# Zero matmuls into spare PSUM columns at the start of an attention and expert kernel

## The chip, the cores and the metric

The kernel runs on one core of a Trainium2 chip. The metric is the device time of one execution in microseconds, and lower is better. Every kernel's result was also compared with the reference; all that are told of here were correct. A run is called slow when it lies over 1.5% above the fastest of the same kernel; comparisons use fast runs. "The clock" of a run is the mean granted TensorE clock in its record, as a share of full speed; the slow start of a run is not in it. In the profiles PE is TensorE (PEld its weight loads), DVE is VectorE, ACT ScalarE, POOL GpSimd and SP SyncE.

## The reference

```python
def _attn_ref(q, k, v, g_q, g_k):           # q, k, v: (8, 12, 448, 64) float32
    def rmsnorm(x, g):
        rms = np.sqrt(np.mean(x * x, axis=-1, keepdims=True) + 1e-06)
        return x / rms * g
    q_n, k_n = (rmsnorm(q, g_q), rmsnorm(k, g_k))
    scores = 1.0 / np.sqrt(64) * np.matmul(q_n, k_n.transpose(0, 1, 3, 2))
    scores = scores - np.max(scores, axis=-1, keepdims=True)
    attn = np.exp(scores)
    attn = attn / (np.sum(attn, axis=-1, keepdims=True) + 1e-09)
    return np.matmul(attn, v).astype(np.float32)

def _moe_ref(x, w_in, w_out):               # x: the attention's output as (3584, 768)
    h = x @ w_in                            # w_in (768, 2048)
    g = h * np.clip(h + 3.0, 0.0, 6.0) / 6.0
    return (g @ w_out).astype(np.float32)
```

## The kernel before

A plan lists steps with estimated durations and dependencies, sorts them greedily, and the program is then written out in that order, each engine in its own fixed sequence. A step that names only one engine is wrapped in a function without a name of its own.

```python
    def add(self, on, dur, due, fn, *deps, ...):
        on, f = ({on: dur}, lambda e: fn()) if isinstance(on, str) else (on, fn)
        s = Step(on, due, f, deps, ...)
# ...
    S_r = Ring(tiles("S", 2, [128, 2, 512], FP32, psum))     # scores: four banks
    X_r = Ring(tiles("X", 1, [128, 512], FP32, psum))        # values: columns 0 to 389
    R_r = Ring(tiles("R", 1, [128, 512], FP32, psum))        # values of the last 64 rows, three pairs of heads
    M_r = Ring(tiles("M", 2, [128, 512], FP32, psum))        # transposes and the expert layers
# ... for the pair of heads P: first two transposes (k, q) on TensorE, each followed by a DVE copy
                tr.append(add("PE", 0.4, at - 2, trans, sc[i], id_make, *mwar))
            ks = add("DVE", 0.45, at - 1, lambda: nc.vector.tensor_scalar_mul(
                kp[:, 0:S], pt[:, 0], gp[:, 0:1]), tr[0], g_make, one_make, *kwar)
            qc = add("DVE", 0.45, at - 1, lambda: nc.vector.tensor_copy(out=kq[:, 1], in_=pt[:, 1]), tr[1], *war)
# ... then four score steps, exponentials on ScalarE, and the value steps into X and R
        X, war, x_use = X_r.take()
        av = []
        for s in range(NS):
            av.append(add("PE", 0.27, at + 0.15 * step * s, lambda s=s: values(
                X[:, s * 130:(s + 1) * 130], s * 128, s == 0), *exps, vc, *war))
# ...
        rest = add("PE", 0.27, at + 0.45 * step, lambda: values(
            Rt[:, i * 130:(i + 1) * 130], S - 128, i == 0), *exps, vc, *war)
# ...
        def norm():                          # the normalisation: DVE reads X
            nc.vector.reciprocal(out=rd[:].unsqueeze(3), in_=xv[:, :, :, D:E1])
            nc.vector.tensor_tensor(out=xn[:], in0=xv[:, :, :, 0:D],
                                    in1=rd[:].unsqueeze(3).to_broadcast([128, NS, 2, D]), op=MULT)

        xe = add("DVE", 0.85, at + 0.5 * step, norm, *av, *dwar, *nwar)
# ... R is read by norm_rest after every third pair; xn is transposed on TensorE, copied to xT by DVE,
# ... and after six pairs the expert matmuls of the batch start
    with tc.manual_schedule():
        for s in plan.order():
            s.fn(s.eng)
```

Below, "kp" and "kq" are DVE's copies of a pair's transposed k and q, and "xn" is its normalised output; a "score pair" is the two score matmuls of one step.

Of the kernel before, what the change touches and what calls it, by code (L numbers as in the profile page):

```python
# [9 lines left out]
BF16 = mybir.dt.bfloat16  # L10
# [134 lines left out]
def kernel(  # L145
# [11 lines left out]
    nc = tc.nc  # L157
# [15 lines left out]
    const = ctx.enter_context(tc.tile_pool(name="const", bufs=1))  # L173
    psum = ctx.enter_context(tc.tile_pool(name="psum", bufs=1, space=PSUM))

    def tiles(name, n, shape, dt=BF16, pool=const):
        return [pool.tile(shape, dt, name=f"{name}{i}") for i in range(n)]

    gq_t, gk_t, gp = (const.tile([128, 1], FP32, name=n) for n in ("gq_t", "gk_t", "gp"))
    mark = const.tile([1, 1], FP32, name="mark")  # L180
    ident = const.tile([128, 128], BF16, name="ident")
    w_in_sb = const.tile([128, NKT, DFF], BF16, name="w_in_sb")
    w_out_sb = const.tile([128, NFT, DM], BF16, name="w_out_sb")
# [19 lines left out]
    X_r = Ring(tiles("X", 1, [128, 512], FP32, psum))  # L203
    R_r = Ring(tiles("R", 1, [128, 512], FP32, psum))
# [58 lines left out]
    def make_ones():  # L263
# [7 lines left out]
        out=gp[:], in0=gq_t[:], scalar=8.0, in1=gk_t[:], op0=MULT, op1=MULT), g_load, after=7.5)  # L271
# [366 lines left out]
    for _, fn in sorted(blocks, key=lambda x: x[0]):  # L638
        fn()

    with tc.manual_schedule():
        for s in plan.order():
            s.fn(s.eng)


# [28 lines left out]
```

## Time and profile before

| | before |
|---|---|
| median of the timed runs | 442.79 us (442.28 to 442.87) |
| profiled execution | 440.47 us, span 438.6 us, clock 1.0 |
| TensorE slow (score pair 0.55 us) | until about 25.5 us |
| first expert matmul | 45.48 us |

Two lines of the page of the kernel before: the busy time of each engine, and the chain of work that ended last, by engine.

```profile
PE 410.6 (94%) x3663; PEld 229.2 (52%) x3682; DVE 246.3 (56%) x417; ACT 249.0 (57%) x425; POOL 240.2 (55%) x230
...
PE 80%; POOL 5%; DVE 4%; ACT 3%; issue 3%; DMA 3%; SPq 1%; POOLq 0%
```

Averages over the span say that TensorE bounds the kernel, and from about 57 us on it does. The first 50 us are another stage, and what sets the pace there has to be read from the timelines of the engines in that stage. The prediction shows those lines.

### The profile page before, as it was taken

The numbers are of one execution on the slowest core, as the hardware profiler recorded it, in microseconds if no ns is written. First come the engines' busy times: TensorE is split into PE (matmuls) and PEld (weight loads), VectorE is DVE, ScalarE is ACT, GpSimd is POOL, SyncE is SP. The second block draws the span as 40 slices with busy tenths as digits, with TensorE's granted clock in tenths as the row PEclk, the third lists the DMA queues.
The fourth block names the chain that finished last, engine by engine and source line by source line (L and its number), as shares of the span: only waits on it lengthen the run. The fifth ranks groups of instructions, "written<-read, shape, count | busy, mean of one in ns | idle before, by whom it ended". The sixth has DMA issues, their size and how long they took to land.

```text
span 438.6 us, 9205 instructions
## 1 busy us (share of the span) xinstructions
PE 410.6 (94%) x3663; PEld 229.2 (52%) x3682; DVE 246.3 (56%) x417; ACT 249.0 (57%) x425; POOL 240.2 (55%) x230
## 2 busy tenths in 40 slices
PE   0588799999999999999999999999999999999995
PEld 0355455555455565554455565554455555654563
DVE  1998887657674564456555465556564444334421
ACT  3788588657765666367664677357673665123200
POOL 3499988855757567656765657747757510000000
PEclk9999999999999999999999999999999999999999
DMA  8999999877545745674465655684465420220122
GB/s 241 247 265 261 224 214 193 216 197 192 128 121 148 189 113 136 167 214 111 133 156 157 177 135 145 159 214 109 120 161 164 97 56 12 54 81 0 37 72 73
DMA packets 102923, 64.58 MB, mean 147 GB/s; under 512 B 59744, under 2 KB 99424, under 8 KB 102880
## 3 DMA queue, kind: packets, MB, share of 16 engines
q1 hardware_dynamic: 94544, 57.01, 50.6%
q0 software_dynamic: 7296, 6.29, 9.1%
q10 hardware_dynamic: 1040, 0.69, 0.5%
q8 instruction: 29, 0.48, 0.5%
q14 instruction: 14, 0.11, 0.1%
HBM read 45.61 MB, written 11.01 MB: 129 GB/s over the span
## 4 chain that ended last, share of the span: by engine, by line
PE 80%; POOL 5%; DVE 4%; ACT 3%; issue 3%; DMA 3%; SPq 1%; POOLq 0%
PE M L558 27%; PE M L533 25%; PE S L416 9%; PE X L437 8%; PE S L558 4%; PE R L437 2%; PE S L533 2%; DVE ssq L337 1%; ACT e L421 1%; POOL qks L351 1%; PE X L558 1%; POOL sq L322 1%; POOL va L359 1%; DMA gq_t<-in_g_q_dram 1%; POOL sq L329 1%
## 5 line engine op out<-in xcount | busy, mean ns | idle before, releaser
L421 ACT ACTIVATE e<-S 112x896 bf16<-112x896 f32 x192 | 166.3, 914 | 64.1 <-PE S L416 64.0
L533 PE MATMUL M<-xT,w_in_sb 128*128 128x384 bf16 (+1 forms) x679 | 145.1, 349 | 3.7 <-DVE gT L541 2.9
L351 POOL TENSOR_TENSOR qks<-qk,rs 112x512 bf16<-112x512 f32 x87 | 90.5, 1055 | 86.6 <-ACT rs L344 84.7
L558 PE MATMUL M<-w_out_sb,gT 128*128 128x384 bf16 x736 | 131.8, 326 | 0.0
L558 PEld LDWEIGHTS <-gT 128*128 128x128 bf16 x896 | 82.9, 98 | 57.8 <-issue 7.8
L533 PEld LDWEIGHTS <-w_in_sb 128*128 128x128 bf16 x768 | 69.6, 97 | 67.4 <-issue 12.5
L541 DVE SCALAR_TENSOR_TENSOR gT<-t,M 128x384 bf16<-128x384 f32 (+1 forms) x116 | 70.6, 611 | 59.1 <-ACT t L539 58.3
L539 ACT ACTIVATE t<-M 128x384 f32<-128x384 f32 (+1 forms) x116 | 62.6, 540 | 67.0 <-PE M L533 65.5
L437 PEld LDWEIGHTS <-e 112*128 112x128 bf16 x1536 | 65.1, 99 | 31.4 <-issue 16.0
L337 DVE TENSOR_REDUCE ssq<-sq 112x16 f32<-112x1024 f32 (+1 forms) x49 | 58.4, 1193 | 23.3 <-POOL sq L329 12.2
L329 POOL TENSOR_TENSOR sq<-qk 112x1024 f32<-112x1024 f32 x36 | 68.1, 1892 | 0.0
L416 PE MATMUL S<-kq,kp 64*128 64x448 bf16 x384 | 56.6, 364 | 4.1 <-DVE kp L381 1.7
L437 PE MATMUL X<-va,e 112*128 112x65 bf16 x1152 | 58.6, 196 | 0.8 <-ACT e L421 0.6
L566 DVE COPY y<-M 128x384 f32<-128x384 f32 x46 | 25.6, 556 | 59.2 <-PE M L558 59.0
L359 POOL CAST va<-vf 112x512 bf16<-112x512 f32 x48 | 31.5, 658 | 10.4 <-DMA vf<-in_v_dram 10.1
L392 POOL TENSOR_SCALAR kp<-kq,gp 128x448 bf16<-128x448 bf16 x23 | 32.3, 1402 | 5.3 <-DMA kq<-qks 5.2
L463 DVE TENSOR_TENSOR xn<-X,rd 128x384 bf16<-128x384 f32 x48 | 26.8, 558 | 1.6
L416 PEld LDWEIGHTS <-kp 64*128 64x128 bf16 x384 | 12.2, 94 | 27.7 <-issue 18.0
L437 PE MATMUL R<-va,e 112*128 112x65 bf16 x384 | 20.4, 195 | 0.0
L377 PE MATMUL M<-ident,qks 112*128 112x112 bf16 x80 | 7.9, 242 | 13.0 <-DVE qks L351 12.4
L558 PE MATMUL S<-w_out_sb,gT 128*128 128x384 bf16 x112 | 19.5, 326 | 0.0
L462 DVE RECIPROCAL rd<-X 128x6 f32<-128x6 f32 x48 | 9.2, 192 | 15.3 <-PE X L437 15.2
(42 smaller groups left out, 156.2 us busy)
## 6 DMA issues: line engine op xcount, KB each, us to landing
qk<-in_k_dram SPq DMA_DIRECT2D x48, 224.0 KB, 3.3
vf<-in_v_dram SPq DMA_DIRECT2D x48, 224.0 KB, 3.7
qk<-in_q_dram SPq DMA_DIRECT2D x45, 224.0 KB, 3.4
w_in_sb<-in_moe_w_in_dram POOLq DMA_DIRECT2D x4, 768.0 KB, 11.3
w_out_sb<-in_moe_w_out_dram POOLq DMA_DIRECT2D x4, 768.0 KB, 11.9
out_dram<-y SPq DMA_DIRECT2D x8, 336.0 KB, 3.1
out_dram<-y SPq DMA_DIRECT2D x8, 288.0 KB, 3.4
out_dram<-y SPq DMA_DIRECT2D x8, 240.0 KB, 3.2
```

Source lines behind the costliest of these rows:

```text
L329: parts = [add("POOL", 1.93, at - 10, lambda: nc.gpsimd.tensor_tensor(out=sq[0:PT], in0=qk[0:PT], in1=qk[0:PT], op=MULT), *ld, *war, lock= ...
L337: red = add("DVE", 0.6 * n, at - 8 * hurry + 0.5 * i0, lambda i0=i0, i1=i1, cs=cs: nc.vector.tensor_reduce(out=ssq[0:PT, cs], in_=sq[0:PT, ...
L351: sc.append(add(on, 0, at - 6 * hurry, lambda e, i=i, rs4=rs4: engines[e].tensor_tensor(out=qks[0:PT, i].rearrange("p t h d -> p h t d"), ...
L359: vc = add({"POOL": 0.61}, 0, at - 3, lambda e: engines[e].tensor_copy(out=va[0:PT, :, :, 0:D], in_=vf[0:PT].rearrange("p h (t d) -> p h t ...
L392: nc.vector if e == "DVE" else nc.gpsimd).tensor_scalar_mul(
L416: nc.tensor.matmul(out=ps[:, a, 0:S], lhsT=kp[rows, c0:c0 + 128], rhs=kq[rows, 1, :], start=True, stop=True)
L421: x = add("ACT", 0.93, at + step * (t0 + i) / T + 0.2, lambda t=t0 + i, ps=ps: nc.scalar.activation(out=e[0:PT, t], in_=ps[0:PT, :, 0:S], ...
L437: nc.tensor.matmul(out=dst[:, a * E1:(a + 1) * E1], lhsT=e[0:PT, t, a, c0:c0 + 128], rhs=va[0:PT, a, t, :], start=(first and a == 0 and t ...
L533: nc.tensor.matmul(out=m[:, 0:n], lhsT=w_in_sb[:, kt, f * 128:(f + 1) * 128], rhs=X[:, kt, :], start=(kt == 0), stop=(kt == NKT - 1))
L539: r = add("ACT", 0.08 + n / 1200, due + span, lambda: nc.scalar.activation(out=t[:, 0:n], in_=m[:, 0:n], func=RELU, bias=0.5, scale=1.0 / ...
L541: g = add("DVE", 0.12 + n / 960, due + span, lambda: nc.vector.scalar_tensor_tensor(out=G[:, f, :], in0=t[:, 0:n], scalar=1.0, in1=m[:, 0: ...
L558: nc.tensor.matmul(out=m[:, 0:HALF], lhsT=G[:, f, i * 128:(i + 1) * 128], rhs=w_out_sb[:, f, cols], start=(f == 0), stop=(f == NFT - 1))
```

## The change

The intent: TensorE starts at half clock and gets the full one only at about 25 us. Zero matmuls into columns of X and R that nobody reads keep it busy from the first instruction on, so that the clock is released before the first real work; more of them, in front of the first 36 TensorE steps, are to keep it released. The destination is meant to be whichever of X and R was read longer ago.

```diff
+    zero = const.tile([128, 120], BF16, name="zero")
...
+    IDLE = [74, 1, 6, 1, 3, 1, 1, 2, 9, 2, 1, 2, 1, 1, 2, 1, 1, 2, 1, 2, 1, 1, 1, 1, 1, 1, 1, 1, 1, 1,
+            1, 1, 1, 1, 1, 1]
+    read = {"norm": [X_r.bufs[0], 0.0], "norm_rest": [R_r.bufs[0], 0.0]}
+
+    def spin(n):
+        to = min(read.values(), key=lambda x: x[1])[0]
+        for _ in range(2 * n):
+            nc.tensor.matmul(out=to[0:120, 392:512], lhsT=zero[:], rhs=zero[:], start=True, stop=True)
+
     with tc.manual_schedule():
+        nc.vector.memset(zero[:], 0.0)
+        n = 0
         for s in plan.order():
+            if s.eng == "PE":
+                if n < len(IDLE):
+                    spin(IDLE[n])
+                n += 1
+            if s.fn.__name__ in read:
+                read[s.fn.__name__][1] = s.end
             s.fn(s.eng)
```

## The prediction

> **What bounds the kernel now.** I read the page's chain first: most of it is dense TensorE work in the perceptron part (L533 and L558 carry 52% between them), and busy time by stretches gives PE 238.07 of 240 us from 60 to 300 us. A start-up effect is therefore worth what it moves the moment, near 56 us, at which that dense work begins; nothing later can win it back, and nothing later can lose more. So the second view is the timeline of PE over the first 30 us (columns: start, duration, engine, line, operation, count, and in brackets the idle time before it and who ended it).
>
> ```profile
> PEclk9999999999999999999999999999999999999999
> ```
>
> ```profile
> 11.69 0.55 PE L377 MATMUL M<-ident,qks 112*128 112x112 bf16 x4 [11.69 <-DVE qks L351]
> ...
> 14.28 0.93 PE L416 MATMUL S<-kq,kp 64*128 64x448 bf16 x4 [1.23 <-DVE kq L383]
> ...
> 19.44 0.55 PE L416 MATMUL S<-kq,kp 64*128 64x448 bf16 x2 [1.67 <-DVE kp L381]
> ...
> 22.88 0.93 PE L377 MATMUL M<-ident,qks 112*128 112x112 bf16 x8
> ...
> 27.19 0.36 PE L416 MATMUL S<-kq,kp 64*128 64x448 bf16 x2
> 27.48 0.37 PE L377 MATMUL M<-ident,qks 112*128 112x112 bf16 x4
> ```
>
> The same pair of score matmuls takes 0.55 us until about 25.5 us and 0.36 us after it; sixteen value matmuls start 0.98 us before their successor early and 0.61 us late. PE is slow until 25.5 us, although the page's clock row shows full clock throughout. From 19.44 to 25.5 PE has no gap over 0.15 us, so it looks like the bound there. The third view, the timeline of DVE over the same time, says otherwise.
>
> ```profile
> 12.36 1.21 DVE L337 TENSOR_REDUCE ssq<-sq 112x16 f32<-112x1024 f32 x1
> 13.49 0.44 DVE L381 TENSOR_SCALAR kp<-M,gp 128x448 bf16<-128x448 bf16 x1
> ...
> 16.17 2.55 DVE L322 TENSOR_TENSOR sq<-qk 112x512 f32<-112x512 f32 x1
> 18.64 0.38 DVE L383 COPY kq<-M 128x448 bf16<-128x448 bf16 x1
> ...
> 23.29 0.56 DVE L463 TENSOR_TENSOR xn<-X,rd 128x384 bf16<-128x384 f32 x1
> 23.85 0.45 DVE L381 TENSOR_SCALAR kp<-M,gp 128x448 bf16<-128x448 bf16 x1
> 24.22 0.38 DVE L383 COPY kq<-M 128x448 bf16<-128x448 bf16 x1
> 24.77 0.36 DVE L480 COPY xT<-M 128x384 bf16<-128x384 bf16 x1 [0.17 <-PE M L476]
> ...
> 27.04 0.20 DVE L462 RECIPROCAL rd<-X 128x6 f32<-128x6 f32 x1 [0.42 <-PE X L437]
> 27.27 0.56 DVE L463 TENSOR_TENSOR xn<-X,rd 128x384 bf16<-128x384 f32 x1
> 27.89 0.39 DVE L383 COPY kq<-M 128x448 bf16<-128x448 bf16 x1
> ```
>
> DVE runs from 12.36 to 24.6 us without a marked gap, and what it takes from PE lay ready before. In the whole cold stretch it waits for PE for 0.17 + 0.42 us. A fast PE can return about 0.6 us there, and no more. From 32.3 us POOL takes over (busy 15.04 of 15.5 us between 29.5 and 45 us); its first link hangs on DVE's reduction at 30.55 us through ScalarE.
>
> **What the Trainium skill says.** "TensorE: Matmul & The Clock Gate", Part 1: TensorE's default clock is half rate, and about 3.4 us of sustained activity, in a free-running window, releases it. The durations agree: the change comes some 6 us after PE's first unbroken stretch begins at 19.44 us. The same page, under Fast Weight Load, has the fast load only with 128 weight columns; the added loads have 120, those of before all 128, so this trace cannot say what a 120-column load costs. "PSUM — Partial Sum Buffer", on bank collisions: two engines may not touch one bank and quadrant at once, even in disjoint columns. So the zeros in X's spare columns are not free of X's readers. "SBUF — State Buffer", Who interferes with whom: an exclusive shared port of DVE and GpSimd; the 2.55 us square at 16.17, against 0.68 us at 35.19, with GpSimd squaring beside it, fits, and it says that DVE's stretch isn't shortened by PE.
>
> **The change part by part.** The list sums to 130, so 260 pairs of weight load and 120-column matmul are added to PE, and one DVE memset of a zero tile. Nothing is removed.
>
> First, 148 pairs from about 1 us. From the 112-column transposes I take cold pairs at (0.55 - 0.295)/3 = 0.085 to 0.11 us (0.295 us is the mean duration of one), say 0.10 at 120 columns, and warm ones at (0.37 - 0.214)/3 = 0.052, say 0.053. If the clock is released about 4.5 us after the start, 45 are cold and 103 warm: 4.5 + 5.5 = 10 us, ending near 11 us. The first transposes start at 11.69, and DVE wants them only at 13.49 us; with fast transposes an end up to 12.6 us costs nothing.
>
> Second, 48 pairs in front of steps 2 to 9 (11.7 to 19.4 us). They fall mostly in gaps of 0.26, 1.23, 0.54 and 1.67 us; up to 19.39 us the chain is DVE's. Cost and gain: about 0.
>
> Third, 64 pairs in front of steps 10 to 36, in the stretch where PE is dense. There cold PE work of 6.06 us shrinks to some 3.6 us, a gain of 2.4 us of PE time; the zeros give back 64 x 0.053 = 3.4 us. Alone this makes PE about as late at 29 us as before: the possible 0.6 us of gain is eaten.
>
> Fourth, new waits. I compared the order of the two built programs with their semaphore values. The intent is to write whichever of X and R was read longest ago, but all 260 go to X: the bookkeeping looks for a function name that the plan's wrapper hides. The program then makes two zero matmuls wait for a normalisation (reciprocal and multiply, DVE) that reads X. Both sit in front of real work.
> (a) The zeros before the third pair's q transposes wait for the first normalisation, which ends at 23.29 + 0.56 = 23.85 us. Before, these transposes ended at 23.81 us. Now: 23.91, two zeros to 24.02, four transposes to their end at 24.39. DVE's kp, in the program behind these transposes, starts at about 24.4 instead of 23.85: DVE stands 0.55 us. The score step behind them starts near 24.43 instead of 23.75.
> (b) The zeros before the third pair's third score step wait for the second normalisation. Carrying (a) on: kq ends 25.2, scores at 25.3; a transpose, sixteen and eight value matmuls and one score pair with five pairs of zeros end at 27.7 us (27.0 before), so the normalisation runs 27.7 to 28.5. Scores at 28.65 instead of 27.19, transposes at 29.05 instead of 27.48, DVE's kq at 29.46 instead of 27.89 us: 1.57 us late, DVE standing some 0.95 us.
> No later zero matmul has a wait. The reduction of 30.55 and POOL's product of 32.33 us follow that kq in order, so POOL's packed stretch starts some 1.5 us late. From there POOL and then PE have little slack; I allow 0.2 us recovered in DVE's small waits for PE between 35 and 40 us (0.44 and 0.27 us). Sum: +1.3 us, 442.8 + 1.3 = 444.1 us.
>
> **The rivals.**
> A: the warm-up works as meant. For it: PE is gapless and slow from 19.44 to 25.5. Against it: DVE's timeline and the two waits. It would be 442.8 - 0.6 = 442.2, and 440 us only if all 2.4 us of PE time lay on the chain.
> B: the 120-column load isn't fast and a pair takes 0.10 us warm as well. Then the first 148 end at 1 + 14.8 = 15.8 us; q's transposes end near 16.4, DVE's kp comes 2.9 us late, and the later zeros cost up to 64 x 0.047 = 3 us more: 447 to 449 us. Against it: 148 x 0.074 us fills exactly the 11 us available, as if tuned with cheap pairs.
> C: the delay is absorbed between 32 and 56 us, because the loads gain 1.5 us on the compute. For it: DMA is full in the first slices. Against it: no wait for DMA is listed for an engine between 29.5 and 60 us. Result 442.8 us.
>
> **Range and chances.** My steps give 444.1 with some 0.6 us of doubt in how much of 1.5 us passes through; A and C stretch the low end to 442.2, a part of B the high end to 446.6. Two per cent is 8.9 us: faster would need 434 us, out of reach even if all slow PE time vanished; slower would need 451.6, above B. Chances: faster 0.01, within 2% 0.97, slower 0.02.
>
> **What would show it.** Right: score pairs of 0.36 us from the first one at 14.28 us; zeros ending between 10 and 12.6 us; DVE's kp of 13.49 us unmoved; a zero matmul ended by DVE's xn, near 23.9 and near 28.5 us; kp of 23.85 at about 24.4 and kq of 27.89 near 29.5 us with PE as its releaser; POOL's product of 32.33 near 33.8 us; the same dense part afterwards, shifted. Wrong: the first transposes after 12.6 us (B), kq near 27.5 us (A), POOL at 33.8 but the first dense stretch at 56 us unmoved (C), or score pairs at 0.55 us still, which would mean that zero operands or the gaps don't hold the clock; then the zeros before 19.4 us cost nothing but those after it twice as much, about 446 us.

## The result, and the profile after

The changed kernel took 446.53 us (median of four runs, 445.91 to 448.24) against 442.63 us before (442.28 to 442.87): 3.9 us slower where 1.3 had been predicted. A ratio here is the mean time of one kernel's fast runs over that of the other's of the same rounds, so not quite the ratio of the medians: 1.0095, 95% interval 1.0066 to 1.0124. Within 2%, and slower beyond doubt. All outputs are right.

The timeline of DVE in the changed kernel (columns as in the prediction):

```profile
12.61 0.16 DVE L271 SCALAR_TENSOR_TENSOR gp<-gq_t,gk_t 128x1 f32<-128x1 f32 x1 [0.43 <-DMA gk_t<-in_g_k_dram]
...
14.41 0.44 DVE L382 TENSOR_SCALAR kp<-M,gp 128x448 bf16<-128x448 bf16 x1
...
25.35 0.45 DVE L382 TENSOR_SCALAR kp<-M,gp 128x448 bf16<-128x448 bf16 x1 [0.56 <-PE M L378]
...
29.08 0.20 DVE L463 RECIPROCAL rd<-X 128x6 f32<-128x6 f32 x1 [0.95 <-PE X L651]
...
30.97 0.39 DVE L384 COPY kq<-M 128x448 bf16<-128x448 bf16 x1 [1.10 <-PE M L378]
```

The two stalls behind waiting zeros are there: 0.56 us before the third pair's kp (0.55 predicted), and 1.10 us before the fourth pair's kq. A third, 0.95 us, is the second normalisation waiting for a zero matmul (L651) that the program put before it (it waited 0.42 us for PE before the change too). And the first kp, which was to stay at 13.49 us, comes at 14.41: DVE waited for the small load gk_t. The timeline of PE in the same run:

```profile
0.97 10.65 PE L651 MATMUL X<-zero 128*120 128x120 bf16 x148 [0.97 <-DVE zero L654]
...
24.85 0.27 PE L651 MATMUL X<-zero 128*120 128x120 bf16 x2 [0.68 <-DVE xn L464]
...
29.92 0.27 PE L651 MATMUL X<-zero 128*120 128x120 bf16 x2 [0.62 <-DVE xn L464]
...
47.81 0.50 PE L477 MATMUL M<-ident,xn 128*128 128x128 bf16 x3 [1.52 <-DVE xn L464]
48.24 0.93 PE L417 MATMUL S<-kq,kp 64*128 64x448 bf16 x4
49.10 4.02 PE L534 MATMUL M<-xT,w_in_sb 128*128 128x384 bf16 x12
```

The first batch took 10.65 us (10 estimated) and both waiting zeros are ended by DVE's xn. The last line is a surprise: twelve expert matmuls took 4.02 us, where the kernel before took 2.12. The page's clock row of the changed kernel, in 40 slices, shows TensorE back at a lower clock in the fifth slice (44 to 55 us):

```profile
PEclk9999699999999999999999999999999999999999
```

In fine windows it was at half clock from 47.1 to 53.9 us. Lining up the same five instructions in both profiled executions gives the whole difference of their spans, 5.5 us:

| instruction | before, us | after, us | late by | added since the line above |
|---|---|---|---|---|
| first pair's kp | 13.49 | 14.41 | 0.92 | 0.92 |
| fourth pair's kq | 27.89 | 30.97 | 3.08 | 2.16 |
| POOL's product after it | 32.33 | 35.50 | 3.17 | 0.09 |
| first expert matmul | 45.48 | 49.10 | 3.62 | 0.45 |
| second group of them | 49.17 | 54.37 | 5.20 | 1.58 |
| end of the span | 438.6 | 444.1 | 5.5 | 0.3 |

Three candidates besides the predicted waits: the late start (0.9 us), more time for the zeros themselves (2.16 us is more than the 1.57 that the waits were to make), and the half clock near 48 us (some 2 us). One profile of each kernel can't say which of them belong to the change.

### The profile page after: what moved, and what is told of

Same layout as the page of the kernel before. It is cut to its first block, busy times and chain, and to the rows that moved or that the text cites. A ratio compares the mean times of both kernels' runs of the same rounds, so it can differ in the third digit from the quotient of the medians.

```text
span 444.1 us, 9726 instructions
## 1 busy us (share of the span) xinstructions
PE 427.2 (96%) x3923; PEld 246.3 (55%) x3942; DVE 245.3 (55%) x418; ACT 249.3 (56%) x425; POOL 241.0 (54%) x230
## 4 chain that ended last, share of the span: by engine, by line
PE 83%; DVE 6%; DMA 3%; ACT 3%; POOL 3%; issue 2%; SPq 0%; POOLq 0%; DVEq 0%
PE M L559 27%; PE M L534 27%; PE S L417 9%; PE X L438 8%; PE S L559 4%; PE S L534 2%; PE R L438 2%; DVE ssq L338 2%; ACT e L422 2%; DMA qk<-in_k_dram 2%; PE X L559 1%; POOL qks L352 1%; DVE qks L352 1%; DVE sq L323 1%; POOL sq L330 1%
## 5 line engine op out<-in xcount | busy, mean ns | idle before, releaser
L534 PE MATMUL M<-xT,w_in_sb 128*128 128x384 bf16 (+1 forms) x679 | 147.0, 352 | 3.6 <-DVE gT L542 2.8
L417 PE MATMUL S<-kq,kp 64*128 64x448 bf16 x384 | 55.5, 357 | 2.7 <-DVE kp L382 0.8
L417 PEld LDWEIGHTS <-kp 64*128 64x128 bf16 x384 | 12.2, 94 | 25.5 <-issue 18.2
L651 PE MATMUL X<-zero 128*120 128x120 bf16 x260 | 23.3, 239 | 2.3 <-DVE xn L464 1.3
L651 PEld LDWEIGHTS <-zero 128*120 128x120 bf16 x260 | 19.5, 151 | 5.0 <-issue 4.0
```

The source lines that it names most:

```text
L417: nc.tensor.matmul(out=ps[:, a, 0:S], lhsT=kp[rows, c0:c0 + 128], rhs=kq[rows, 1, :], start=True, stop=True)
L534: nc.tensor.matmul(out=m[:, 0:n], lhsT=w_in_sb[:, kt, f * 128:(f + 1) * 128], rhs=X[:, kt, :], start=(kt == 0), stop=(kt == NKT - 1))
L651: nc.tensor.matmul(out=to[0:120, 392:512], lhsT=zero[:], rhs=zero[:], start=True, stop=True)
```

## The experiments

Three theories were told apart: the **waits** (zeros that wait for a reader of X), the **start** (early zeros make the first loads late) and the **throttle** (TensorE falls back to half clock near 48 us). All 18 kernels were timed in five rounds; medians are of six runs. Line numbers of the kernels differ by a few lines. Where the time of a clock change is given to a hundredth, it is an entry of the clock record in the packed trace.

### First group: parts of the change alone

**e1_fix_names** mends the bookkeeping, so that 44 of the 260 zeros go to R as intended and none waits.

```diff
         on, f = ({on: dur}, lambda e: fn()) if isinstance(on, str) else (on, fn)
+        f.__name__ = fn.__name__
```

Expected:

> The bookkeeping mended, so that 44 of the 260 zero matmuls go to R and none waits for a normalisation. Waits theory (the two waits on X's readers are the loss): the q transposes of the third pair follow k's at once, DVE's kp has no wait of 0.56 us there, kq of the fourth pair comes 1.2 to 1.6 us earlier than in the changed kernel (30.97 us there); time 1.2 to 1.6 us below the changed kernel, 444.9 to 445.4 us. Start theory (the first loads are late by 0.9 us because of the added work): DVE's first kp stays near 14.4 us (13.49 before). Throttle theory (TensorE slows again near 48 us, which costs 2 us): a stretch 45 to 60 us at a granted clock below 1 stays, and the time falls by less than 1 us.

Measured: 444.53 us (443.41 to 445.89), before in this group 443.08 (440.80 to 444.86); ratio 1.0044 (1.0016 to 1.0073). The time lies just below the 444.9 to 445.4 us of the waits theory, though not in the same rounds as the first result. The trace does not bear the theory out: the fourth kq came 16.6 us after the first kp, no earlier than in the changed kernel (also 16.6), and a normalisation waited 2.40 us for zeros in X. It held a surprise. Windows of 3.41 us, with the busy time of PE, PEld, DVE, ACT and POOL, and after them the granted clock:

```profile
8.68:12.09 3.41, 2.53 (x47) 2.40 (x44) 1.86 (x3) 2.56 (x8) 1.92 (x3) 1.00 0.99 194
12.09:15.50 3.41, 1.52 (x22) 1.35 (x23) 2.60 (x7) 1.79 (x5) 0.51 (x1) 0.99 1.15 213
15.50:18.91 3.41, 3.30 (x21) 1.92 (x21) 3.41 (x4) 1.79 (x2) 3.40 (x5) 0.50 1.12 297
```

After a window in which PE was busy for 1.52 of 3.41 us the clock fell to half, and it stayed there to 22.3 us. The warm-up was lost before the dense stretch began.

**e2_first_only** has only the first 148 zeros (`IDLE = [74]`). Expected:

> Only the first 148 zero matmuls, none later. Waits theory: with no wait and no zeros in the dense stretch the time falls to 442.2 to 442.8 us, a little under or equal to before, as DVE sets the pace; score pairs are 0.36 us from the first or fall back to 0.55 if sparse work lets the clock drop. Start theory: first loads still land late, kp near 14.4 us, so 443.3 to 443.7 us. Throttle theory: the slow stretch near 48 us stays in the trace and the time stays over 444 us.

Measured: 441.81 us (440.21 to 443.96), ratio 0.9982 (0.9948 to 1.0016): not told apart from before. The first kp came at 14.44 us; the clock was at half from 16.0 to 26.3 us, and again from 46.7 to 50.1. Score pairs fell back to 0.55 us, which the expectation had allowed. The late kp is as the start theory had it, the time is not (443.3 to 443.7 us), and the half clock near 48 us was there without the 444 us of the throttle theory.

**e3_to_step9** has the zeros of steps 1 to 9 and not the 64 later ones (`IDLE` cut after nine entries). Expected:

> The zeros up to step 9 (148 and 48), none of the 64 later ones. Waits theory: as the run with the first 148 only, 442.2 to 442.8 us; score pairs at 0.36 us all through. Start theory: 443.3 to 443.7 us. Throttle theory: over 444 us, with the granted clock below 1 between 45 and 60 us.

Measured: 452.8 us in the median, five of six runs at 452.8 to 453.7 and one at 444.15, so the profiled one counts as slow, and no ratio is given. Neither theory had this. The timelines of DVE and then of POOL in that (slow) execution:

```profile
29.27 4.73 DVE L352 TENSOR_TENSOR qks<-qk,rs 112x512 bf16<-112x512 f32 x1
```

```profile
28.87 1.04 POOL L352 TENSOR_TENSOR qks<-qk,rs 112x512 bf16<-112x512 f32 x1
29.87 1.03 POOL L323 TENSOR_TENSOR sq<-qk 112x512 f32<-112x512 f32 x1
30.85 0.60 POOL L360 CAST va<-vf 112x512 bf16<-112x512 f32 x1
31.42 2.03 POOL L323 TENSOR_TENSOR sq<-qk 112x512 f32<-112x512 f32 x2
```

A DVE product that takes 0.69 us elsewhere took 4.73: it came 0.4 us after GpSimd began a row of five instructions, and ended 0.6 us after that row did. In the kernel before the same product was asked for at 28.20 us and took 1.22. So a shift of some tenths of a microsecond may change who gets past whom; no run tests that. In the three traces with the whole change (the first, e6 and e12) no DVE product of the first 70 us takes over 2.55 us, so this is not part of its loss.

**e4_two_waits** has only the two pairs of zeros that wait (`IDLE` zero but for a 1 at steps 17 and 27), no warm-up. Expected:

> Only the four zero matmuls in two places that wait for a normalisation, no warm-up (TensorE slow until 25.5 us as before). Waits theory: DVE's kp waits 0.6 to 0.8 us near 24.5 us, the third pair's third scores come after the second normalisation, kq of the fourth pair near 29.5 to 30 us (27.89 before), time up by 1.2 to 2 us: 443.8 to 444.6 us. Start theory: first loads as before, kp at 13.49 us, time up by no more than 0.3 us. Throttle theory: unchanged time unless the granted clock falls below 1 near 48 us; if it does, up by 2 us.

Measured: 443.45 us (441.17 to 446.79), ratio 1.0022 (0.9979 to 1.0064): inconclusive by time. In the trace, of the slowest of its six runs, DVE's third kp waited 0.83 us for PE, and the fourth kq came 17.2 us after the first kp (14.4 before). TensorE stayed at half clock until 36.32 us, not 25.5 as expected, so this stretch does not show the waits alone.

### Second group: a control, the noise, and no waits

**e5_before_again** is the kernel before against itself. Expected:

> The kernel before against itself. Throttle theory (TensorE is set back to half clock near 48 us in most runs of any kernel, each window of 3.4 us of it costs about 1.7 to 2 us): runs with a mean clock of 1.0 take 440.5 to 441.5 us, runs at 0.996 take 443 to 443.5, at 0.992 near 445; the time follows the clock. Start theory: with no zeros the first kp comes at 13.5 to 13.8 us in this second trace too. If kp comes at 14.4 us or later here, the late start is chance and not the zeros.

Measured: 442.97 us, ratio 1.0006 (0.9984 to 1.0029). The eleven base runs of this group span 440.35 to 443.96 us, and the time mostly follows the clock: 440.35 and 440.93 at 1.0, most others 442.5 to 444 at 0.990 to 0.996. The trace shows where. The timeline of PE in this second profile of the unchanged kernel:

```profile
44.73 0.34 PE L476 MATMUL M<-ident,xn 128*128 128x128 bf16 x3 [1.52 <-DVE xn L463]
45.01 0.55 PE L416 MATMUL S<-kq,kp 64*128 64x448 bf16 x4
45.49 3.71 PE L533 MATMUL M<-xT,w_in_sb 128*128 128x384 bf16 x12
```

The kernel before has the half clock near 48 us too, and its first profile was one of the minority without it: of the 51 executions of it in these groups 15 have a clock of 0.998 or more. So those 2 us of the profiles' difference are not the change's, and two profiles alone would have misled. The first kp came at 13.50 us.

**e6_after_again** is the changed kernel once more. Expected:

> The changed kernel once more, for a second trace on the chip of the control. Waits theory: kp of the third pair waits 0.5 to 0.9 us, kq of the fourth pair comes 1.9 to 2.3 us later, counted from the first kp, than in the kernel before (14.40 us there). Start theory: first kp near 14.4 us again. Throttle theory: mean clock 0.983 to 0.991, so two to four windows of 3.4 us; time 446 to 448 us.

Measured: 445.36 us (443.11 to 447.98), ratio 1.0053 (1.0011 to 1.0095). First kp at 15.12 us; the clock fell at 15.3 us and returned at 22.1; the fourth kq came 18.0 us after the first kp (16.6 in the first trace), the late dense stretch of half-clock zeros being added to the waits: DVE's first normalisation alone stood 2.20 us for zeros in X.

**e7_r_only** sends all 260 zeros to R, which has no reader before step 36.

```diff
-        to = min(read.values(), key=lambda x: x[1])[0]
+        to = R_r.bufs[0]
```

Expected:

> All 260 zeros to R, which nothing reads before step 36: neither the zeros nor the normalisations wait for one another. Waits theory: as the run with mended names, 444 to 445 us, 1.5 to 2.5 us below the changed kernel; kq of the fourth pair 14.9 to 15.2 us after the first kp (14.40 before, 16.56 in the changed kernel). If the zeros' own time were the loss and not the waits, it would stay at 446 to 447 us. Throttle theory: if TensorE falls to half clock near 15 us, the zeros in the dense stretch take twice as long and the gain is lost.

Measured: 444.29 us (443.12 to 445.23), ratio 1.0032 (1.0008 to 1.0056). No zero waits any more, yet it is slower than before: the zeros cost something of their own. The clock fell at 14.2 us, and the fourth kq came 16.4 us after the first kp, where the waits theory had 14.9 to 15.2.

**e8_fill_gap** is the kernel before, with 26 zeros in one place only: behind the sixth pair's R values, into R, where TensorE otherwise stands for 1.52 us (`IDLE` is empty).

```diff
+        def rest_values():
+            values(Rt[:, i * 130:(i + 1) * 130], S - 128, i == 0)
+            if P == 5:
+                for _ in range(26):
+                    nc.tensor.matmul(out=R_r.bufs[0][0:120, 392:512], lhsT=zero[:], rhs=zero[:], start=True, stop=True)
-        rest = add("PE", 0.27, at + 0.45 * step, lambda: values(
-            Rt[:, i * 130:(i + 1) * 130], S - 128, i == 0), *exps, vc, *war)
+        rest = add("PE", 0.27, at + 0.45 * step, rest_values, *exps, vc, *war)
```

Expected:

> The kernel before with only 26 zero matmuls to R, in the idle 1.5 us of TensorE between the sixth pair's R values and its transposes (43.2 to 44.7 us), where nothing waits for them. Throttle theory: no half clock near 48 us, mean clock 1.0 in nearly all runs, time 440.5 to 441.5 us, 1.5 to 2.5 us below the median of before. If the throttle near 48 us isn't set off by this gap, the clock stays at 0.994 to 0.996 and the time at 443 us.

Measured: 439.91 us (439.64 to 441.52), ratio 0.9942 (0.9919 to 0.9965), clock 0.998 to 1.0. The timeline of PE:

```profile
44.28 1.61 PE L456 MATMUL R<-zero 128*120 128x120 bf16 x26
45.96 0.34 PE L482 MATMUL M<-ident,xn 128*128 128x128 bf16 x3
46.24 0.55 PE L417 MATMUL S<-kq,kp 64*128 64x448 bf16 x4
46.72 2.12 PE L539 MATMUL M<-xT,w_in_sb 128*128 128x384 bf16 x12
```

This beats both kernels, and it is a quiet base: with the half clock near 48 us gone, the parts of the change can be measured on it.

### Third group: the change, part by part, on the quiet base

**e9_fill_again** is that base.

> The kernel before with the 26 zeros in the gap near 44 us, again, as the quiet base of this group: 439.6 to 441.5 us, clock 0.998 to 1.0, 2 to 3 us below before. First kp between 13.5 and 14.2 us.

**e10_fill_first** adds the first 148 zeros (`IDLE = [74]`).

> That base with the first 148 zeros. Start theory (the zeros delay the first loads by about 0.9 us): first kp at 14.4 us or later and 0.7 to 1.2 us above the base. If the late start is chance or is absorbed: within 0.4 us of the base. Warm-up as intended would be 0.6 us or more below the base; I expect none, as TensorE falls back to half clock near 15 us and DVE sets the pace.

**e11_fill_r_only** adds all 260, all to R.

> That base with all 260 zeros, all to R, so no waits. Zeros theory (the zeros themselves, run partly at half clock, cost as much as the waits): 1.5 to 2.5 us above the base. Waits theory (only the waits cost): within 1 us of the base.

**e12_fill_full** adds the change as it is.

> That base with the whole change as it is (all zeros to X, two waits). Waits theory: 1.4 to 1.7 us above the run with all zeros to R. Altogether 3 to 4 us above the base, 443 to 444 us; if the half clock near 48 us were the main loss of the change, this would lie within 1.5 us of the base.

| kernel | median, us | range | above the base (medians) | difference of means, 95% interval |
|---|---|---|---|---|
| e9: base | 440.55 | 440.10 to 440.88 | | |
| e10: + first 148 | 441.39 | 440.16 to 444.02 | 0.84 | 1.4 ± 1.7 |
| e11: + all 260, to R | 442.95 | 441.65 to 443.61 | 2.40 | 2.3 ± 0.8 |
| e12: + change as it is | 444.48 | 442.98 to 445.50 | 3.93 | 3.7 ± 1.0 |
| before, same chip | 442.70 | 440.35 to 443.96 | | |

The whole change costs 3.9 us on this base, as much as in the first result. The waits, e12 less e11, are 1.5 us by the medians (1.4 ± 1.1 by the means); the zeros without any wait are 2.4 us (2.3 ± 0.8). How those divide between the first 148 and the 112 later ones (0.84 and 1.56 by the medians) is not clear of the scatter.

### Fourth group: which zeros, and does a held clock pay?

**e13_fill_third** is the base again: 440.04 us (439.07 to 441.14).

> The base of this group (26 zeros in the gap near 44 us, nothing else): 439.9 to 440.6 us, clock 0.998 to 1.0, first kp 13.5 to 14.2 us.

**e14_fill_dense** has the base and only the 64 zeros of steps 10 to 36, to R (`IDLE` with nine zeros in front).

> That base with only the 64 zeros of steps 10 to 36, to R. TensorE is at half clock there until about 25.5 us, so the first 44 zeros cost about 0.1 us each. If the dense zeros are the cost of the later zeros: 1.5 to 3 us above the base. If the zeros of steps 2 to 9 are: within 0.5 us of the base. First kp as in the base.

Measured: 444.02 us (443.21 to 445.47), 4.1 ± 1.0 us above its base (means). The timeline of DVE, at the three longest of its waits for a TensorE that is held up by zeros:

```profile
26.23 0.45 DVE L382 TENSOR_SCALAR kp<-M,gp 128x448 bf16<-128x448 bf16 x1 [1.04 <-PE M L378]
...
29.83 0.20 DVE L468 RECIPROCAL rd<-X 128x6 f32<-128x6 f32 x1 [0.82 <-PE X L438]
...
31.10 0.39 DVE L384 COPY kq<-M 128x448 bf16<-128x448 bf16 x1 [0.48 <-PE M L378]
```

The zeros in the dense stretch are dear: without the warm-up (the clock was released at 24.55 us) they cost as much as the whole change does. Not all that the trace shows is theirs, though: its first kp came at 14.40 us, 1.31 us later than in the base's trace, without any early zero and against the expectation. From there to the fourth kq it took 16.7 us, 13.8 in the base.

**e15_fill_short** has the base and 40 early zeros (`IDLE = [20]`), over at 5.2 us.

> That base with only 40 zeros at the start, over by about 5 us. If the late start comes with any early work of TensorE: first kp at 14.4 us or later and 0.5 to 1 us above the base. If it takes the whole 148: first kp 13.5 to 14.2 us, and the time of the base within 0.3 us.

Measured: 441.30 us (440.51 to 442.08), 1.25 ± 0.8 us above its base. The first kp came at 14.02 us, in the range of the second expectation, but the time is that of the first: even 40 zeros, long over before anything needs TensorE, cost something.

**e16_fill_hold** tries the warm-up as it should be: longer fillers up to step 9, none in the dense stretch (`IDLE = [78, 10, 12, 1, 5, 1, 1, 2, 17]`).

> That base with longer fillers up to step 9 (156, 20, 24, 2, 10, 2, 2, 4, 34 zeros) and none later. If they hold the clock: no half clock from 8 us on in the trace, score pairs of 0.36 us throughout. Prediction's DVE bound: then at most 0.6 us below the run with the first 148 alone, so 440.8 to 441.5 us (0.2 to 1 us above the base because of the late start). Warm-up as intended (TensorE's 2.4 us are on the chain): 1 to 2 us below the base. If DVE and GpSimd fall out of step[...] as in the run with the zeros to step 9: near 448 us with one DVE product of over 3 us.

Measured: 442.09 us (441.10 to 445.57), 2.5 ± 1.8 us above its base. The clock was full from the release to 26.3 us, as wanted. The timelines of DVE and of PE:

```profile
14.30 0.44 DVE L382 TENSOR_SCALAR kp<-M,gp 128x448 bf16<-128x448 bf16 x1
...
24.59 0.44 DVE L382 TENSOR_SCALAR kp<-M,gp 128x448 bf16<-128x448 bf16 x1
...
27.71 0.20 DVE L468 RECIPROCAL rd<-X 128x6 f32<-128x6 f32 x1 [0.64 <-PE X L438]
```

```profile
24.73 0.34 PE L482 MATMUL M<-ident,xn 128*128 128x128 bf16 x3 [1.48 <-DVE xn L469]
...
26.56 0.56 PE L417 MATMUL S<-kq,kp 64*128 64x448 bf16 x2
```

From the first to the third pair's kp it took 10.29 us with TensorE at full clock throughout; in the kernel before, with TensorE at half clock, 10.36, and in the base e13 10.28. In this stretch a fast TensorE bought nothing: it finished early and stood 1.48 us for DVE. Worse, standing there it lost its clock at 26.3 us, and then DVE did have to wait for it.

### Fifth group: the waits alone on the base

**e17_fill_waits** has the base and the two waiting pairs.

> The base with the gap filled, and only the two pairs of zeros that wait for a normalisation, at half clock. Waits theory, as the prediction worked it out: 1.2 to 2.2 us above the base, DVE's kp of the third pair some 0.6 to 0.9 us and kq of the fourth pair 1.5 to 2.8 us later after the first kp than in the base. If the waits cost only together with the other zeros: within 0.5 us of the base.

**e18_fill_fourth** is the base.

> The base: 439.9 to 440.6 us, clock 0.998 to 1.0, about 0.5% below the kernel before for the fourth time; first kp between 13 and 14.4 us.

Measured: 442.27 us (440.22 to 446.21) against 439.97 (439.25 to 441.00): 2.3 us by the medians, 2.8 ± 2.5 by the means. Two pairs of zeros, four matmuls in all, cost something when they wait for another engine; the scatter forbids a sharper figure. In the trace, again of one of the slower runs, the fourth kq came 17.2 us after the first kp (13.9 in the base's trace). The timeline of PE shows that this is not the waits alone:

```profile
33.05 0.56 PE L417 MATMUL S<-kq,kp 64*128 64x448 bf16 x2
...
34.91 0.36 PE L417 MATMUL S<-kq,kp 64*128 64x448 bf16 x2
```

TensorE was at half clock until 34.93 us, as it was in e4 until 36.32; the traces of the kernel before and of its base were released between 22.60 and 28.40 us. That the stands before the zeros put the release off is likely and not shown. The changed kernel, released at 6.12 us, doesn't pay this, so e12 less e11 is the better measure of its waits. The base was below the kernel before for the fourth time: 0.9942, 0.9951, 0.9956 and 0.9961, each interval below 1 (the first two share most of their runs of the kernel before).

## Why the prediction was right or wrong

- **DVE, not TensorE, sets the pace up to 24 us:** right, and shown by e16 (10.29 us against 10.36). The gain of at most 0.6 us that it allowed was not seen in the time of any run, but it is in the traces, after 24 us: where TensorE had its full clock early, by chance in e13 and e18 (released at 22.60 and 23.53 us) or back in e10 (24.46), the fourth kq came 13.8 to 13.9 us after the first kp, against 14.4 in the kernel before (25.85) and 15.1 in e8 (28.40).
- **The zeros themselves, the first three parts of the sum, together 0: this is the term that failed.** Without any wait they cost 2.3 ± 0.8 us (e11 less e9). The times don't settle how this divides: the first 148 are 1.4 ± 1.7 us (e10 less e9; on the kernel before, e2, nothing could be told), the rest 0.9 ± 1.8. The traces show two places.
- **The first 148:** their length was right (10.65 us, against 10). "An end up to 12.6 us costs nothing" held for the zeros themselves. But the first kp did not stay at 13.49 us. With early zeros it came at 13.96 to 15.12 us in eleven traces (mean 14.54), without them at 13.07 to 14.65 in nine (mean 13.78): a tendency of 0.8 us with overlapping ranges. In ten of the eleven DVE waits for the small load gk_t (0.35 to 1.11 us), but so it does in four of the nine (0.34 to 0.49 us). Why early zeros should make that load late, no run shows; this stays open. The time agrees for 40 zeros (1.25 ± 0.8 us).
- **The 48 zeros of steps 2 to 9, "about 0", and the 64 in the dense stretch, which were to leave PE "about as late at 29 us as before":** without waits the fourth kq came 16.4 and 16.2 us after the first kp (e7, e11), against 14.4 before (13.8 to 15.1 in the six traces of the kernel before and its base). Two sizes were wrong. The zeros were sized by their rate in a long row, 0.053 us; between unlike steps two of them add 0.12 to 0.16 us at full clock, and between 24 and 33 us of the changed kernel the chain of work lies on zeros for 36.9% of the time. And the 2.4 us of TensorE time set against them took for granted that the clock, once released, holds. In eight of the nine traces with the first 148 zeros (e16 left out, which has longer fillers) it had fallen again by 16 us and came back between 18.75 and 26.23. TensorE had been busy for 0.54 to 1.52 of the 3.41 us before; the profile of the changed kernel happened to be the ninth, where the windows lay otherwise and the one in that place had 2.19 us of work. Whether the late start brought the falls about was not tested, and the loss doesn't need them: in the ninth the fourth kq was late all the same.
- **The two waits:** right in place, and in size as far as the scatter lets one see. The stall of kp was 0.56 us (0.55 predicted). The whole effect is 1.4 ± 1.1 us (e12 less e11), where 1.57 less 0.2 had been predicted; that the middle hits so well is in part luck. Counted from the first kp, the fourth kq was late by 2.16 us instead of 1.57 in the changed kernel; the slower zeros are the likely difference. The allowance of 0.2 us recovered between 35 and 40 us did not come: POOL's product kept the whole delay (3.08 us became 3.17).
- **Rival A** fell: the warm-up gained no time in e16, where it held up to 26.34 us. **Rival B** fell: pairs at full clock took 0.055 us (mean from start to start, 6.2 to 11.6 us of the changed kernel). **Rival C** fell: in the two profiles the delay reached the expert matmuls whole (3.17 us became 3.62).
- What neither theory nor rival had: the half clock near 48 us, which, to judge by their clocks, most executions of the kernel before have as well. It inflates the difference of the two profiles by some 2 us, and isn't a cost of the change.
- A reading that was off without consequence: sixteen value matmuls early start 1.00 us before their successor on the timeline, not 0.98.

So the mechanism of the waits was right, and the sum was too small by the term for the zeros: predicted 0, measured 2.3 ± 0.8 us.

## What to carry to other kernels

A dense, slow TensorE is worth speeding up only if its consumer waits for it: here DVE had no gap up to 24 us, and a TensorE at full clock merely stood idle and lost its clock again. Filler work must go where the engine really idles, to a bank that nobody reads meanwhile (R is read at 45.94 us in e8, just after the zeros): 26 zeros in one 1.5 us gap gained 0.5%, while 260 spread over the start cost 0.9%. And profile the unchanged kernel more than once: its first trace was one of the minority without a throttled stretch, and comparing it with one trace of the change would have blamed the change for 2 us of noise.

## What the Trainium skill lacked or had wrong

- "TensorE: Matmul & The Clock Gate", Part 1 and the closing table: it puts the fall back to half clock down to a wholly idle window of about 3.4 us, and warns of gaps over 3 us. Its section on psum-queue cycling has a clock that swings through short idles, without a length. Here gaps of about 1.5 us were enough. In the eleven traces examined, the 3.41 us before the fall had TensorE busy for 0.45 to 1.92 us; in the window before that one, where the clock held, it was busy for at least 2.53 us. Two examples, in e5 and in the filled e8 (same stretch; the clock fell in the first and held in the second):

```profile
42.49:45.90 3.41, 1.89 (x28) 1.13 (x27) 3.27 (x7) 2.17 (x3) 3.41 (x4) 0.99 1.21 269
```

```profile
42.49:45.90 3.41, 3.15 (x59) 2.59 (x59) 3.18 (x6) 2.24 (x5) 3.41 (x4) 1.00 1.12 283
```

- What no page gives is the share of work that holds the clock. With windows laid from each trace's own first release in steps of 3.413 us, over the first 70 us of the twenty traces: all thirteen with at most 1.61 us of TensorE work were followed by half clock, none with 2.03 us or more was, and between 1.80 and 1.94 both happened. The kernel before had 1.89 us in its window from 42.92 to 46.33 us and kept its clock, e5 had 1.89 us from 42.44 to 45.85 and lost it, so the busy time alone does not decide there.
- The same page, Part 1: that the window is free-running agrees. The first release came at another time in each trace (22.60 to 28.40 us for the kernel before and its base), and half-clock stretches after it lasted whole windows: 3.41, 6.83, 10.24 or, in e15, 17.07 us. The page does not say that zero operands release and hold the clock as real ones do; here rows of zeros did: in e15, where they ended before a release, 40 zeros took 4.26 us (0.107 us each), and in e16, after it, a row of 34 took 2.08 us (0.061 us each).
- The same page, Fast Weight Load and LDWEIGHTS: its formula, 120 columns over 1.2, gives an estimate of 100 ns for a load that is not fast. The 120-column loads lasted 164 ns on average in the first batch of the changed kernel and 135 in e8, at full clock (98 for 128 columns in the expert layers), but a load with its matmul took 0.055 us in a row at full clock: the load's duration did not bound the rate.
- No page says that the record of the granted clock begins only with the first release and that the views read full until then: in the kernel before its first entry is at 25.85 us, and the views show 1.00 before that, with score pairs of 0.55 us instead of 0.36.
- "SBUF — State Buffer", Who interferes with whom: it says that the engine that comes first keeps the shared port for its whole instruction and the other is blocked; it does not say who comes next. In e3 (a slow run) a DVE product lasted through five GpSimd instructions in a row, 4.73 us.
